# Attention scores as two 54-row passes on the two row halves of the matmul array, instead of one 110-row pass on the whole array

## The chip, the core and the metric

The kernel runs on one core of a Trainium2 chip. TensorE (PE) multiplies matrices, VectorE (DVE), ScalarE (ACT) and GpSimd (POOL) work on the results, SyncE (SP) issues most DMAs. The metric is the device time of one execution in microseconds (us). Smaller is better.

## What is computed

Two independent parts share the inputs' size (2048 positions, 576 features), and their outputs stand side by side:

```
# A: attention, 32 heads of 18 features, 4 segments of 512 positions
for s in range(4):
    logits = einsum("bhqd,bhkd->bhqk", q[s], k[s]) * 18**-0.5 + mask   # causal, within the segment
    a_dot  = einsum("bhqk,bhkd->bhqd", softmax(logits), v[s])
    a_mem  = (phi(q[s]) @ M) / (phi(q[s]) @ z + 1e-6)                  # M, z: sums over earlier segments
    out[s] = g * a_mem + (1 - g) * a_dot
    M += phi(k[s]).T @ v[s];  z += phi(k[s]).sum()
A = out @ wo
# B: a 2-D Fourier filter
B = irfft2(rfft2(x) * (w_r + 1j * w_i))
```

## The kernel before

The program is one stream per engine, in the order in which the Python code records it (a manual schedule). First come the forward transform of B and the projections to q, k and v; then the inverse transform of B, with the first steps of the attention in between (`prologue`); then the attention (`attention`), which takes the second half of the time.

For precision each value of q and k is held as three bf16 numbers (high, middle, low), and six of their nine products are kept. So a head's dot product over 18 features becomes one over 6 x 18 = 108 rows: `Qs` and `Ks` are tiles of 108 rows by 8 heads by 512 positions, and a matmul contracts all 108 rows. They are read back from DRAM by `stack_dmas`, three DMAs for a tile. Two more rows, 108 and 109, hold the maximum of each query (high and low part) and, on the key side, -1.

A *quad* is four heads of one segment; there are 32 quads (`k` = 0 to 31), and each takes four steps `t` of the attention loop, one per head. A step of the loop records these pieces, in this order:

- `s1` (line 688, the *maxima*) for a head 11 steps ahead: queries times keys over 108 rows into a PSUM tile of the pool `ps1` (three buffers, tag `s1`; while no background work asks for the buffer `post`, every fourth tile goes there), which DVE reads with the mask added and reduces to one maximum per query (line 692). A head has 1280 columns: one tile with 384 + 128 columns, one with 512, and every second head one with 256 + 256 for two heads.
- `s2` (lines 725 to 735, the *scores*): keys times queries, transposed, over 110 rows, so that the maximum is already subtracted, into one of three buffers `s2`; ACT takes the exponential (lines 726, 731, 736) into `P`. Also 1280 columns a head. Its matmuls alternate with those of `s1`.
- `run_bg`: one unit of background work at a time (`den`, `mixed`, `combine`, `mem1`, `oproj`: the memory part, the division, the output projection with `wo`), on the whole array, between two pieces of `s1` and `s2`.
- `pv` (line 763): the exponentials times the values, in fp32, four heads side by side on four column quarters of the array; a quad's products stand in two blocks, one in every second step, or for six quads in one block.
- `mpath`: in the steps 0 and 1 of a quad the maxima of the quad after next are split into high and low (POOL), transposed (PE, line 709, `mt`), copied (ACT), and sent by one DMA of ACT's queue into rows 108 and 109 of `Qs` (line 715).

PE's instructions wait in order for their semaphores; an instruction that waits holds up what stands behind it.

## Time and profile before

| | us |
|---|---|
| median of 3 runs (lowest, highest) | 673.66 (672.79, 673.68) |
| the profiled execution | 673.47 |
| its span, first to last instruction | 671.8 |
| PE busy | 658.6 (98%) |
| DVE busy | 543.2 (81%) |
| ACT busy | 440.6 (66%) |
| POOL busy | 189.6 (28%) |

The table's first rows are times of whole executions; the span is what the profile covers. A busy share is the union of an engine's instructions. Since matmuls are pipelined, the duration of one holds some fixed latency beside its streaming, so that a PE that is 98% busy can still lose time between matmuls; starts of neighbouring matmuls tell more than their durations.

### The profile page before, as it was taken

How to read it: one execution, taken by the hardware profiler on the slowest of the kernel's cores; microseconds unless marked ns; L12 is line 12 of the kernel's file. 1: busy time of each engine (PE TensorE's matmuls, PEld its weight loads, DVE VectorE, ACT ScalarE, POOL GpSimd, SP SyncE). 2: the span in 40 equal slices, each digit the busy share in tenths (PEclk: the TensorE clock that was granted, in tenths of full speed). 3: DMA queues.
4: the chain of work that ended last, by engine and by line, in shares of the span. 5: the costliest groups of instructions: out<-in, count | busy, mean ns of one | idle time of the engine just before them, and what ended most of it. 6: DMA issues, size and time to landing. Idle time of an engine off the chain costs nothing.

```text
span 671.8 us, 14143 instructions
## 1 busy us (share of the span) xinstructions
PE 658.6 (98%) x4776; PEld 484.3 (72%) x4776; DVE 543.2 (81%) x1514; ACT 440.6 (66%) x900; POOL 189.6 (28%) x387
## 2 busy tenths in 40 slices
PE   9999999999999999999999999999999999998997
PEld 5999779879879878999974454444666445663597
DVE  5998989889889778689769998998856988568643
ACT  3886796576487385444449988878756787567521
POOL 2111000100200012456506543445323564133410
PEclk9999999999999999999999999999999999999999
DMA  9896466497388478799545885876667576332152
GB/s 339 306 310 195 124 185 206 143 300 233 89 239 266 132 231 266 223 264 289 168 134 157 219 218 152 204 219 182 166 165 204 135 200 161 99 113 79 35 171 75
DMA packets 76034, 127.57 MB, mean 190 GB/s; under 512 B 12812, under 2 KB 44202, under 8 KB 72370
## 3 DMA queue, kind: packets, MB, share of 16 engines
q1 hardware_dynamic: 69310, 110.67, 57.3%
q0 software_dynamic: 5632, 15.76, 8.2%
q8 instruction: 37, 0.61, 0.4%
q10 hardware_dynamic: 1020, 0.25, 0.2%
q14 instruction: 35, 0.29, 0.1%
HBM read 81.78 MB, written 43.92 MB: 187 GB/s over the span
## 4 chain that ended last, share of the span: by engine, by line
PE 86%; DVE 5%; ACT 3%; DMA 3%; issue 2%; POOL 1%; SPq 0%; ACTq 0%; DVEq 0%; POOLq 0%
PE pj L487 15%; PE pv L763 11%; PE s L688 10%; PE pjv L487 7%; PE po L916 5%; PE i L331 4%; PE i L320 4%; PE f L145 4%; PE s L725 4%; PE c L166 4%; PE s L729 3%; PE pn L837 2%; PE s L735 2%; PE po L946 2%; PE pm L559 2%
## 5 line engine op out<-in xcount | busy, mean ns | idle before, releaser
L692 DVE CUSTOM_DVE_ANT_0 junk<-s,x 128x384 bf16<-128x384 f32 (+3 forms) x512 | 219.1, 486 | 42.2 <-PE s L688 39.7
L738 POOL TENSOR_SCALAR_AFFINE_SELECT P<-P 128x512 f32<-128x512 f32 (+2 forms) x135 | 80.6, 620 | 51.6 <-ACT P L726 47.3
L726 ACT ACTIVATE P<-s 128x512 f32<-128x512 f32 x128 | 76.7, 599 | 20.6 <-PE s L725 17.6
L763 PE MATMUL pv<-P,vs 128*32 128x512 f32 (+3 forms) x1024 | 81.0, 438 | 0.0
L731 ACT ACTIVATE P<-s 128x512 f32<-128x512 f32 x128 | 76.2, 596 | 3.4 <-PE s L730 3.0
L763 PEld LDWEIGHTS pv<-P,vs 128*32 128x32 f32 x1024 | 27.2, 109 | 44.0 <-issue 39.9
L688 PE MATMUL s<-Ks,Qs 108*128 108x512 bf16 (+3 forms) x256 | 57.7, 300 | 1.0 <-DVE mg L692 0.4
L487 PE MATMUL pj<-x,wqkh 128*128 128x512 f32 x162 | 56.1, 408 | 0.0
L232 DVE TENSOR_TENSOR Z<-Z 128x580 f32<-128x580 f32 (+2 forms) x51 | 45.9, 913 | 0.6
L692 DVE DVE_READ_ACCUMULATOR2_ANT mg<- 128x1 f32 x512 | 42.5, 83 | 0.0
L548 POOL MEMSET vt<- 128x32 f32 x16 | 2.3, 162 | 139.3 <-PE pm L559 125.5
L320 PE MATMUL i<-civ,Y 128*128 128x256 f32 (+1 forms) x288 | 39.7, 290 | 0.9 <-POOL Y L305 0.9
L736 ACT ACTIVATE P<-s 128x512 f32<-128x512 f32 x64 | 38.7, 605 | 2.5 <-PE s L735 1.1
L688 PEld LDWEIGHTS <-Qs 108*128 108x128 bf16 x320 | 26.9, 98 | 15.6 <-issue 11.0
L320 PEld LDWEIGHTS i<-civ,Y 128*128 128x128 f32 (+1 forms) x288 | 36.8, 181 | 1.9 <-POOL Y L305 1.3
L331 PE MATMUL i<-itab,T 128*128 128x290 f32 (+1 forms) x224 | 36.0, 304 | 0.1
L487 PE MATMUL pj<-x,wqkl 128*128 128x512 f32 x90 | 35.5, 395 | 0.0
L487 PE MATMUL pj<-xh,wqkh 128*128 128x512 f32 x90 | 35.5, 395 | 0.0
L487 PE MATMUL pj<-xh,wqkl 128*128 128x512 f32 x90 | 35.5, 395 | 0.0
L487 PEld LDWEIGHTS pj<-x,wqkh 128*128 128x128 f32 x162 | 30.5, 189 | 6.4
L506 DVE SCALAR_TENSOR_TENSOR ex<-pj,ex 128x512 f32<-128x512 f32 (+1 forms) x28 | 19.3, 689 | 19.5 <-ACT ex L504 19.4
L514 ACT CAST sp<-pj 128x512 bf16<-128x512 f32 x36 | 21.1, 585 | 18.6 <-DVE pj L507 18.4
(209 smaller groups left out, 1694.1 us busy)
## 6 DMA issues: line engine op xcount, KB each, us to landing
qkD<-sp SPq DMA_DIRECT2D x32, 384.0 KB
xin<-xb SPq DMA_DIRECT2D x16, 384.0 KB
cfw<-cfw POOLq DMA_DIRECT2D x16, 384.0 KB, 4.8
civ<-civ POOLq DMA_DIRECT2D x16, 384.0 KB, 8.3
Ks<-qkD SPq DMA_DIRECT2D x12, 512.0 KB
x<-qkD SPq DMA_DIRECT2D x10, 512.0 KB
Qs<-qkD SPq DMA_DIRECT2D x10, 512.0 KB
vs<-vD SPq DMA_DIRECT2D x16, 310.5 KB
```

The costliest lines, as they stand in the source:

```text
L232: s.nc.vector.tensor_tensor(o,a,b,op=op)
L320: nc.tensor.matmul(p[:m,k],Y[i][:,q,c*128:c*128+m],cc[:,hl,o:o+256],start=n==0,stop=n==5)
L331: nc.tensor.matmul(p,x,t,start=n==0,stop=n==6)
L487: s.nc.tensor.matmul(out,a,b,start=i==0,stop=i==len(L)-1)
L688: for o,i,e in J: nc.tensor.matmul(p[:,o:o+128*i+128],Q[:108,h+e,128*i:128*i+128],K[:108,h+e,:128*(i+1)],start=True,stop=True)
L692: nc.vector.tensor_tensor_reduce(out=junk[:,:w],in0=p[:,o:o+w],in1=s.mask[:,512-w:],scale=1.0,scalar=-3.0e38, op0=OP.add,op1=OP.max,accum_ ...
L726: nc.scalar.activation(P[0][:,hh],p0,AF.Exp,scale=SC)
L731: nc.scalar.activation(P[1][:,hh],p1,AF.Exp,scale=SC)
L736: nc.scalar.activation(P[2][:,hh-1:hh+1].rearrange("p h c -> p (h c)"),p2,AF.Exp,scale=SC)
L738: nc.gpsimd.affine_select(out=x[:,a:b],in_=x[:,a:b],pattern=[[0,b-a],[1,128]],compare_op=OP.is_ge,fill=0.0,base=0,channel_multiplier=-1)
L763: nc.tensor.matmul(s.pvt[32*hh:32*hh+32,128*j:],vt[:,152*j+19*h:152*j+19*h+32],mv[0][:,hh,mv[1]],start=j==0,stop=j>1,skip_group_check=True)
L916: nc.tensor.matmul(ps,a[t][:r,c],b[:r,t,w],start=i==0,stop=i==13)
```

## The change

A tile of queries or keys is now 56 rows of one row half of the array and 56 of the other: heads 0 to 3 of a group of eight lie in rows 0 to 55 (half 0), heads 4 to 7 in rows 64 to 119 (half 1). Each head's 108 rows are split in two parts of 54, which lie behind each other in the free dimension. A quad is now two heads of either half.

- The maxima (`fill`) use only one part of 54 rows, that with the leading products, so they are maxima of slightly rougher logits. Tiles are called A (384 + 128 columns), C (512) and B (256 + 256 for two heads); a quad has four A, four C and two B.
- The scores (`scores`, `s2`) take two passes that add up in PSUM: 56 rows (54 and the two of the maximum) and then 54. The exponentials are the same in number and size.
- `seg` replaces the alternation of `s1` and `s2` by a written list for each of the quad's four steps, with maxima of one or two quads ahead.
- `mpath` runs in steps 2 and 3 of the quad in place of 0 and 1, and sends two DMAs (one for each half) in place of one.
- `stack_dmas` issues four DMAs of 4 KB runs in place of three of 8 KB runs, with the same bytes.
- Background units of the output projection are taken two at a time in odd steps (`s.proj`), and `pv` stands in one block for quads 11 to 28. PSUM: four `s2` buffers, which `pv`, `mt`, `pn` and `po` now share, one buffer `x` for the rest, three `s1` buffers as before and none lent to them.
- The prologue does the maxima of two and a half quads in 15 calls (before: two and three quarters in 33).

In the order of PE's instructions the array changes between whole, row halves and column quarters 222 times in the attention (before 122) and 23 times in the inverse stage (before none).

```diff
-        L.append(lambda: nc.sync.dma_start(T[32:96].rearrange("p a c -> p (a c)"),s.qkD[g][u].rearrange("i (d h) c -> (i d) (h c)",h=8)))
...
+        for R in range(2):
+            m=bass.AP(tensor=a.tensor,offset=a.offset+2048*R,ap=[[65536,3],[4096,16],[65536,2],[1,2048]])
+            L.append(lambda R=R,m=m: nc.sync.dma_start(flat(T[64*R:64*R+48]),m))
+        def go(R):
+            m=bass.AP(tensor=e.tensor,offset=e.offset+(8*G+4*R)*512,ap=[[16384,6],[6*16384,2],[1,2048]])
+            nc.sync.dma_start(flat(T[64*R+48:64*R+54]),m)
...
-    def s1(s,t):
...
-            p=s.ps.tile([128,512],F32,name="s1",tag="post") if s.spare and s.n1%4==0 else s.ps1.tile([128,512],F32,name="s1",tag="s1")
-            for o,i,e in J: nc.tensor.matmul(p[:,o:o+128*i+128],Q[:108,h+e,128*i:128*i+128],K[:108,h+e,:128*(i+1)],start=True,stop=True)
...
+    def fill(s,k,kind,x):
+
+        nc=s.nc; n,qd=divmod(k,2); Q,K=s.Qs[n%3],s.Ks[n%4]; tp=s.sm; R=x//2 if kind!="B" else x
...
+        J={"A":[(0,2,x,384),(384,0,x,256)],"C":[(0,3,x,512)],"B":[(0,1,2*x,384),(256,1,2*x+1,256)]}[kind]
+        p=s.ps1.tile([128,512],F32,name="s1",tag="s1"); r=slice(64*R,64*R+54)
+        for o,i,hh,b in J:
+            j=2*qd+hh%2
+            nc.tensor.matmul(p[:,o:o+128*i+128],Q[r,0,j,128*i:128*i+128],K[r,1,j,:128*(i+1)],start=True,stop=True)
...
-        out=Q[108:110,4*qd:4*qd+4].rearrange("p h (i c) -> p (h i) c",c=128)
-        if s.now<0: nc.gpsimd.dma_start(out,mt)
-        else: s.later(2,lambda: nc.scalar.dma_start(out,mt))
+        def send(eng):
+            for R in range(2): eng.dma_start(Q[64*R+54:64*R+56,0,2*qd:2*qd+2].rearrange("p h (i c) -> p (h i) c",c=128),mt[16*R:16*R+16])
+        if s.now<0: send(nc.gpsimd)
+        else: s.later(2,lambda: send(nc.scalar))
...
+    def scores(s,p,n,J):
+
+        Q,K=s.Qs[n%3],s.Ks[n%4]; f=True
+        for b,rows in ((0,56),(1,54)):
+            for i,(o,h,kb,qo) in enumerate(J):
+                R,j=h//4,h%4; r=slice(64*R,64*R+rows)
+                s.nc.tensor.matmul(p[:,o:o+512-qo],K[r,1-b,j,128*kb:128*kb+128],Q[r,b,j,qo:],start=f,stop=b==1,skip_group_check=True)
+                f=False
+    def s2(s,k,kind,x):
+        nc=s.nc; n,qd=divmod(k,2); h=2*qd+(4*x if kind==2 else 4*(x//2)+x%2); tp=s.tp
...
+        p=s.ps.tile([128,512],F32,name="s2",tag="s2")
+        J={0:[(0,h,0,0)],1:[(0,h,1,128),(384,h,3,384)],2:[(0,h,2,256),(256,h+1,2,256)]}[kind]
+        s.scores(p,n,J)
+        nc.scalar.activation(P[2][:,2*x:2*x+2].rearrange("p h c -> p (h c)") if kind==2 else P[kind][:,x],p,AF.Exp,scale=SC)
+    def seg(s,t):
+
+        k,q=divmod(t,4)
+        L=(((0,0),("C",3),(0,2),("A",1)),((1,0),(1,2),("C",1),(2,1),("B",1),("B",0)),
+           ((0,1),("A",2),(0,3),("C",0)),((1,1),(1,3),("A",3),(2,0),("C",2),("A",0)))[q]
+        for a,x in L:
+            if a in (0,1,2):
+                if k<32: s.s2(k,a,x)
+            elif k+2+q//2<32: s.fill(k+2+q//2,a,x)
...
-        one=k in (16,17,18,24,25,26)
+        one=10<k<29
...
-        def run_bg(rate):
+        def run_bg(rate,t=1):
             state["acc"]+=rate
-            if state["acc"]>=1:
+            if t%2==0 and s.proj: return
+            while state["acc"]>=1:
...
-            steps(a,1)
-            steps(b,1)
-            run_bg(0)
-            steps(a,1)
-            steps(b,1)
-            run_bg(s.rate)
-            steps(a,1)
-            steps(b,1)
+            s.seg(t)
+            run_bg(s.rate,t)
             if 4<=t-1<132: s.pv((t-5)//4,(t-5)%4)
-            if hh==1 and m is not None: steps(m,2)
-            if hh==0 and k+2<32: m=s.mpath(k+2); next(m)
+            if hh==3 and m is not None: steps(m,2)
+            if hh==2 and k+2<32: m=s.mpath(k+2); next(m)
...
-                    tp=pool(es,"tp2",2); ps=es.enter_context(PP(tc,"ps",dict(s2=3,pv=1,post=1)))
+                    tp=pool(es,"tp2",2); ps=es.enter_context(PP(tc,"ps",dict(s2=4,x=1)))
```

PE in an early quad, first head of the quad, before (each LDWEIGHTS loads the weights of the MATMUL behind it; L688 is a maximum, L725 to L730 are scores; the last number is output rows x columns):

```order
L688 LDWEIGHTS Qs_3168
L688 MATMUL s_5450<-Ks_3169,Qs_3168 128x384
L688 LDWEIGHTS Qs_3168
L688 MATMUL s_5450<-Ks_3169,Qs_3168 128x128
L725 LDWEIGHTS x_2634
L725 MATMUL s_5457<-Qs_3167,x_2634 128x512
L688 LDWEIGHTS Qs_3168
L688 MATMUL s_5460<-Ks_3169,Qs_3168 128x512
L729 LDWEIGHTS x_2634
L729 MATMUL s_5464<-Qs_3167,x_2634 128x384
L730 LDWEIGHTS x_2634
L730 MATMUL s_5464<-Qs_3167,x_2634 128x128
```

Maxima and scores alternate, and each tile of scores is done by one matmul per 512, 384 or 128 columns. The same place now, the first step of a quad (L720 are scores, L689 maxima; `s_5852` belongs to a head of half 0, `s_5856` and `s_5860` to heads of half 1, `s_5864` to half 0):

```order
L720 LDWEIGHTS Ks_3171
L720 MATMUL s_5852<-Qs_3170,Ks_3171 128x512
L720 LDWEIGHTS Ks_3171
L720 MATMUL s_5852<-Qs_3170,Ks_3171 128x512
L689 LDWEIGHTS x_2634
L689 MATMUL s_5856<-Ks_3172,x_2634 128x512
L720 LDWEIGHTS Ks_3171
L720 MATMUL s_5860<-Qs_3170,Ks_3171 128x512
L720 LDWEIGHTS Ks_3171
L720 MATMUL s_5860<-Qs_3170,Ks_3171 128x512
L689 LDWEIGHTS x_2634
L689 MATMUL s_5864<-Ks_3172,x_2634 128x384
```

Two passes of one head stand directly behind each other on one half; a maximum of the other half follows.

ACT, from the exponentials of one quad (`P_4581`) to those of the next (`P_4737`), now (L708 copies the transposed maxima, L710 sends them):

```order
L710 DMA Qs_3169<-mts 2x8x128 x2
L729 ACTIVATE P_4582<-s_4610 128x512
L729 ACTIVATE P_4582<-s_4616 128x512
L729 ACTIVATE P_4583<-s_4626 128x512
L729 ACTIVATE P_4581<-s_4656 128x512
L729 ACTIVATE P_4581<-s_4668 128x512
L729 ACTIVATE P_4582<-s_4681 128x512
L729 ACTIVATE P_4582<-s_4687 128x512
L729 ACTIVATE P_4583<-s_4700 128x512
L654 CAST woh<-ob 128x576
L708 COPY mts<-mt 32x128
L772 COPY U<-pv 128x512
```

The two DMAs stand 8 exponentials ahead of the quad that needs them; before, the one DMA stood 13 exponentials ahead.

180 lines of the change are left out of this document (71 added, 109 removed).

## The prediction

> **What bounds the kernel now.** I read the page first: its span, the engines' shares, and the chain that ended last.
>
> ```profile
> span 671.8 us, 14143 instructions
> ...
> PE 658.6 (98%) x4776; PEld 484.3 (72%) x4776; DVE 543.2 (81%) x1514; ACT 440.6 (66%) x900; POOL 189.6 (28%) x387
> ...
> PE 86%; DVE 5%; ACT 3%; DMA 3%; issue 2%; POOL 1%; SPq 0%; ACTq 0%; DVEq 0%; POOLq 0%
> ```
>
> PE is the chain. The change touches the attention only, so I cut that by time: five quads without background work, five with light background, three with the output projection, and the end. The edges are starts of the transpose `mt`, one per quad; columns are PE, PEld, DVE, ACT, POOL, clock, DMA share, GB/s.
>
> ```profile
> 364.90:400.30 35.40, 35.40 (x329) 17.56 (x325) 34.04 (x164) 32.60 (x66) 19.57 (x35) 1.00 0.85 223
> 438.50:482.60 44.10, 44.08 (x343) 21.80 (x344) 40.11 (x171) 35.54 (x70) 21.69 (x39) 1.00 0.77 201
> 482.60:520.00 37.40, 37.33 (x327) 24.77 (x325) 23.24 (x101) 23.79 (x50) 11.46 (x26) 1.00 0.62 167
> 611.80:671.80 60.00, 54.73 (x407) 40.41 (x407) 31.24 (x48) 23.07 (x49) 12.06 (x25) 1.00 0.30 93
> ```
>
> A quad takes 7.08, 8.82 and 12.47 us in the first three. From 356.62 to 363.70 below is one of the early ones, 7.08. PE fills all of it; DVE stands at 96%, 91% and 62%. So in the first two there is a second engine close behind PE. How PE spends a quad shows in the timeline (start, duration):
>
> ```profile
> 356.62 1.28 PE L763 MATMUL pv<-P,vs 128*32 128x512 f32 x16
> ...
> 362.73 0.38 PE L725 MATMUL s<-Qs,Ks 110*128 110x512 bf16 x1
> 362.95 0.38 PE L688 MATMUL s<-Ks,Qs 108*128 108x512 bf16 x1
> 363.17 0.33 PE L729 MATMUL s<-Qs,Ks 110*128 110x384 bf16 x1
> 363.34 0.22 PE L730 MATMUL s<-Qs,Ks 110*128 110x128 bf16 x1
> 363.39 0.38 PE L735 MATMUL s<-Qs,Ks 110*128 110x256 bf16 x2
> 363.70 1.28 PE L763 MATMUL pv<-P,vs 128*32 128x512 f32 x16
> 364.92 0.23 PE L709 MATMUL mt<-idb,mh 128*128 128x128 bf16 x1
> 364.99 0.33 PE L688 MATMUL s<-Ks,Qs 108*128 108x384 bf16 x1
> ```
>
> Starts, not durations, give the cost: 512 columns take 0.22 us (362.73 to 362.95), of the 0.38 of a record 0.16 is latency. I call 512 columns a **unit**, 0.218 us. The two 256-column matmuls from 363.39 are one unit and end at 363.61, yet `pv` starts at 363.70: going from the whole array to column quarters costs **0.09**. A half block of `pv` takes 1.22 to the next start. A quad's maxima and scores are 20 units, 4.36; with 2 x 1.22, the first change of each block (2 x 0.09) and `mt` (0.07) that makes 7.05 of the 7.08.
>
> DVE's share in an early quad:
>
> ```profile
> 372.48 0.56 DVE L692 CUSTOM_DVE_ANT_0 junk<-s,x 128x384 bf16<-128x384 f32 x1 [0.19 <-PE s L688]
> ...
> 372.97 0.29 DVE L692 CUSTOM_DVE_ANT_0 junk<-s,x 128x128 bf16<-128x128 f32 x1
> ...
> 373.18 0.69 DVE L692 CUSTOM_DVE_ANT_0 junk<-s,x 128x512 bf16<-128x512 f32 x1
> ...
> 373.79 0.42 DVE L692 CUSTOM_DVE_ANT_0 junk<-s,x 128x256 bf16<-128x256 f32 x1
> ...
> 374.13 0.42 DVE L692 CUSTOM_DVE_ANT_0 junk<-s,x 128x256 bf16<-128x256 f32 x1
> ...
> 374.48 0.55 DVE L692 CUSTOM_DVE_ANT_0 junk<-s,x 128x384 bf16<-128x384 f32 x1
> ```
>
> By the starts a tile A (384 and 128) takes DVE 0.49 + 0.21 = 0.70, C 0.61, B 0.34 + 0.35 = 0.69. A quad (4 A, 4 C, 2 B) is **6.62 us of DVE**, and it was idle for 0.19 ahead of it, once in two heads. The change leaves this work as it is.
>
> **Do two halves run side by side?** No row shows row halves. The nearest is `pv`, four heads on four column quarters:
>
> ```profile
> L763 PE MATMUL pv<-P,vs 128*32 128x512 f32 x256 | 34.1, 605 | 0.0
> L763 PE MATMUL pv<-P,vs 128*32 128x384 f32 x256 | 27.2, 496 | 0.0
> ```
>
> 128 columns more cost 109 ns, so 512 fp32 columns stream in 0.44. There are 256 records for 128 matmuls: each fp32 product is two passes, and in the compiled stream the two passes of a head stand directly behind each other. If a pass that finds its quarter busy held up those behind it, the four heads' passes of 512 and of 128 would take 5 x 0.44 + 5 x 0.11 = 2.7 us. The 16 records from 363.70 take 1.22, twice 0.44 + 0.11 and a change. So the quarters advance independently, and I take the same for row halves.
> [...]
>
> **The change, part by part**, against the profiled execution's 673.5 (span 671.8 and 1.7 around it; the median of the runs, 673.7, is the same).
>
> *Streaming.* In units on half 0 and half 1 the four steps of `seg` hold 3 and 3, 4 and 5, 3 and 3, 5 and 4. Independent halves take 3 + 5 + 3 + 5 = 16 units in place of 20: -0.87 us of PE per quad.
>
> *Changes of the array.* 222 in place of 122 in the attention, about 3 more per quad. Whole to row halves is not shown; from 0 to the 0.09 of the column change. I take 0.09: +0.28 per quad, in projection quads (6 in place of 2) +0.37.
>
> *Feeding DVE.* This decides. Step 1 ends with C, B, B and step 3 with A, C, A, 1.99 and 2.01 us of DVE work, and three `s1` buffers hold just that. After the last of them PE feeds DVE nothing until the next quad's first maximum is complete. In an early quad that spell is 0.22 (last tile) + 0.09 + 1.22 (`pv`) + 0.07 + 0.09 (`mt`) + 0.44 (two passes of scores, which complete first) + 0.16 (latency) = 2.29; after step 1, without `mt`, 2.13. DVE is dry for 0.28 + 0.14 at least; as it has begun on the first tile before the third can be written, rather 0.65. While DVE has all three, PE waits, and the scores behind the waiting maximum wait with it. So an early quad takes between 7.04 and 7.4; I take 7.25: +0.17 for 11 quads (2 to 12), **+1.9**. PE's saving is not seen there, since DVE sets the time.
>
> In light quads (13 of those from 13 on) DVE has 40.11 / 5 = 8.02 busy against 34.04 / 5 = 6.81 before, so 1.2 more than 6.62. `pv` is one block there; two rows of the chain of waits give it and a background unit:
>
> ```profile
> 498.89 1.19 PE po L916 x7
> 500.31 2.29 PE pv L763 x32
> ```
>
> The spell without maxima becomes 0.22 + 0.09 + about 0.5 (a unit; 1.2 for one of `po`, less for `pb`) + 0.09 + 2.29 + 0.16 + 0.44 + 0.16 = 3.95, of which 2.0 is covered: dry 1.95. A quad by this loop: 6.62 + 1.2 + 1.95 = 9.8. PE alone would need 8.82 - 0.87 + 0.28 = 8.2. If part of the 1.2 falls into the dry spell it is 9.0; if PE and DVE wait for each other in turn, 10.4. I take 9.8: +1.0 x 13 = **+13** (ends -8 and +20).
>
> In the six projection quads PE has 12.47 - 0.87 + 0.37 = 12.0 and DVE 7.75 of work: PE sets the time, **-3**.
>
> *Start and end.* The prologue leaves 29.5 quads of maxima to the attention, before 29.25: 6.62 / 4 = **+1.7**. After the last maxima (2.5 quads) scores stand alone, 2 + 4 + 2 + 4 = 12 units in place of 10: 0.44 x 2.5, with the changes **+1.5**.
>
> *Rows of the maxima.* Before, the DMA that carries them left 9.67 us before the first use (the issue in ACT's timeline, the first scores of that quad in PE's):
>
> ```profile
> 373.20 0.62 ACTq L715 DMA_DIRECT2D Qs<-mts  x1
> ```
>
> ```profile
> 382.87 0.38 PE L725 MATMUL s<-Qs,Ks 110*128 110x512 bf16 x1
> ```
>
> Now two leave, 8 exponentials ahead in place of 13: 9.67 x 8 / 13 = 6.0 us, less 0.62 for the second. No wait for it shows today, and none is told of its landing; 0 to 7 us in all, I take **+1**. If the cover is gone, the first pass of every quad waits, and behind it everything on PE.
>
> *At nothing:* the loads of Q and K (same bytes, runs of 4 KB, one DMA more per tile on SP, whose queue waits mostly for the engines), the reordered stores of the projection, ACT's second issue (0.62, running beside an exponential; ACT has 35.40 - 32.60 = 2.8 free in five early quads, so it would cost 0.06 each if it did not overlap), the 23 changes in the inverse stage (2.1, against half or less of the maxima's streaming there).
>
> Sum: 1.9 + 13 - 3 + 1.7 + 1.5 + 1 = +16.1, from 673.5 to **690**.
>
> **Rivals.**
>
> *In order* (15%). A matmul that finds its half busy holds up the next. Then a step overlaps only where the half changes: 4 + 7.25 + 4 + 7.5 = 22.75 units, 0.60 more than before per quad. Early quads 7.08 + 0.60 + 0.09 = 7.77 (+7.6 for 11); light quads PE 8.82 + 0.88 = 9.7 with the loop at 9.8 or above, about 10.2 (+18); projection quads +0.97 each (+6); start, end and rows +4.2: +36, **709**. Against it: the 1.22 of `pv`; for it, that columns are not rows. [...]
>
> *Faster* (11%). The saved units come through: three buffers bridge the gaps, and DVE's other work falls into the dry spells. The point is a dry time below 1.0 us per light quad (8.82 - 7.82). Then early quads stay at 7.08, light ones take 8.82 - 0.87 + 0.37 = 8.3 (-0.5 x 13), the others -3, start and end +3: -6.5, **667**. For it: DVE's 91% and 62%, and the two heads' even spacing of work today; against it: 3.95 of `pv` and background in one piece.
>
> *Rows late* (8%). The DMAs land after their use in every quad of the early and light stretches by 0.4 us more than I took: +9, **699**. For it: two DMAs on queues at 85% DMA share; against it: 6 us.
>
> *No side by side at all* (4%): 30 units in place of 20, +2.18 and the changes for 29.5 quads, +73, **747**.
>
> *No difference* (3%): losses and gains cancel, 673.
>
> **How the numbers follow.** The forecast has 59% and its own range is 681 to 699 (light quads 9.3 to 10.4, early ones 7.04 to 7.4). The range of 8 in 10 reaches to the in-order case: 675 to 712; outside are the faster case, the 747 and half of the in-order case's far end. Below 0.2% (1.3 us) a measurement of this kernel cannot tell a difference. Faster 11%, same 3%, slower 86%.
>
> **What would show it.** Right: early quads of 7.2 to 7.4 (starts of `mt`), light quads of 9 to 10.4, DVE idle before the first maximum of a quad with PE as releaser, PE idle before the last maximum of steps 1 and 3 with DVE as releaser, two records of different halves starting within 0.01 us. Wrong: starts of a maximum only with the second pass ahead of it (in order); light quads below 8.8 (faster); PE waiting for the DMA of the maxima before the first pass of a quad (rows late); a change of whole array to halves that costs nothing would take up to 9 us (100 x 0.09) from the sum.

## The result, and the profile after

The changed kernel takes 727.87 us (median of 4 runs, 725.92 to 731.77) against 673.47 of the kernel before (four runs taken beside it): 1.082 times as long, 95% interval 1.077 to 1.087, or +54 us. The forecast was +16.5 us and a range up to 712, so the direction was right and the size was not. One of the four executions of `rows_by_pool` below lies 2% above its fastest, and its row is the median of the other three.

The page of the changed kernel: span, engines, and the chain of waits by engine and by line.

```profile
span 724.2 us, 15284 instructions
...
PE 682.5 (94%) x5288; PEld 490.1 (68%) x5288; DVE 543.0 (75%) x1514; ACT 432.7 (60%) x900; POOL 191.2 (26%) x389
...
PE 50%; DMA 13%; DVE 7%; ACT 6%; issue 5%; POOL 2%; SPq 1%; ACTq 1%; DVEq 0%; POOLq 0%
PE pj L487 10%; PE pv L766 7%; DMA Qs<-mts 6%; PE pjv L487 6%; PE s L720 6%; PE i L331 4%; PE i L320 4%; DVE junk L693 4%; PE po L912 4%; PE s L689 3%; ACT P L729 2%; DMA x<-mts 2%; PE po L942 2%; PE pm L559 2%; DMA vD<-vt 1%
```

PE was 86% of the chain and is 50%; DMA was 3% and is 13%, and 8% of it are two names that carry the rows of the maxima, `Qs<-mts` and `x<-mts` (the same tile under its first name). To see where the time went I cut both spans at the same starts of `mt`: first to third, third to thirteenth, thirteenth to seventeenth, seventeenth to last. First the kernel before (columns as in the prediction):

```profile
310.10:351.20 41.10, 39.84 (x302) 36.52 (x301) 30.78 (x102) 17.70 (x42) 16.17 (x25) 1.00 0.62 179
351.20:423.40 72.20, 71.31 (x650) 35.22 (x651) 68.03 (x326) 63.54 (x128) 34.15 (x64) 1.00 0.70 192
423.40:456.40 33.00, 32.42 (x273) 15.19 (x269) 31.82 (x138) 27.73 (x56) 16.21 (x34) 1.00 0.81 212
456.40:611.80 155.40, 153.30 (x1267) 88.71 (x1264) 118.44 (x501) 111.02 (x223) 63.80 (x114) 1.00 0.57 152
```

Then the changed one:

```profile
322.80:358.30 35.50, 33.85 (x245) 27.40 (x242) 26.34 (x95) 14.23 (x33) 10.11 (x17) 0.90 0.69 180
358.30:453.60 95.30, 81.06 (x827) 37.83 (x826) 69.73 (x330) 62.96 (x129) 36.38 (x67) 0.91 0.71 144
453.60:497.80 44.20, 36.60 (x339) 16.82 (x335) 33.60 (x142) 27.19 (x57) 17.25 (x34) 0.92 0.72 168
497.80:665.30 167.50, 159.32 (x1504) 89.96 (x1500) 117.29 (x495) 104.91 (x223) 60.61 (x111) 1.00 0.60 139
```

The span grew by 52.4: +7.1 up to the third `mt` (358.3 against 351.2), **+23.1** in the ten early quads, +11.2 in the next four, +12.1 in the last fifteen, and -1.1 in the tail (58.9 against 60.0). Two things are new in the stretches with the largest loss: PE stands still (81.06 busy of 95.30), and the granted clock, the share of full speed that PE was given, is 0.91 where it was 1.00. The intervals between starts of `mt` in the ten early quads are 8.28, 7.55, 11.32, 7.54, 10.87, 7.64, 14.96, 7.55, 12.08, 7.55. So there are two sorts of quad: a good one of 7.55, and a late one of 11 to 15. One late quad in the timeline (ACT's issues and PE):

```profile
367.65 0.62 ACTq L710 DMA_DIRECT2D Qs<-mts  x1
...
368.31 0.62 ACTq L710 DMA_DIRECT2D Qs<-mts  x1
...
374.11 0.23 PE L705 MATMUL mt<-idb,mh 128*128 128x128 bf16 x1
...
376.76 0.39 PE L720 MATMUL s<-Qs,Ks 56*128 56x512 bf16 x1 [2.42 <-DMA Qs<-mts]
```

The rows leave at 367.65 and 368.31, PE is ready for them at 374.34, and goes on at 376.76, 8.45 us after the second issue. The clock follows in the next rows, stretches of 3.4 us around that pause (the shortest pieces at half clock in this trace last 3.41 us):

```profile
371.40:374.80 3.40, 2.70 (x32) 1.15 (x26) 3.13 (x16) 3.14 (x8) 1.91 (x4) 1.00 1.05 165
374.80:378.20 3.40, 1.44 (x17) 0.85 (x18) 0.77 (x3) 1.05 (x3) 1.97 (x3) 1.00 1.03 210
378.20:381.60 3.40, 3.40 (x25) 1.15 (x22) 2.70 (x14) 1.92 (x4) 0.38 (x2) 0.50 0.63 125
381.60:385.00 3.40, 3.16 (x40) 1.69 (x40) 2.53 (x11) 2.67 (x6) 0.98 (x2) 1.00 0.55 159
```

PE was idle for about 2 of the 3.4 us from 374.80, and the next 3.4 us, in which it had work throughout, ran at half the clock. So this pause is followed by a second loss. Seven such pieces, 30.7 us in all, lie between 350 and 490 us, each right behind a pause of 0.85 us or more in the stretch before it; the kernel before has none ahead of its end. Its longest wait of PE between 350 and 500 us is this one (total, times, longest):

```profile
PE mt L709 <- DVE mg L692: 0.9, 1, 0.9
```

### The profile page after: what moved, and what is told of

The parts are those of the page before. It is cut to its first block, busy times and chain, and to the rows that moved or that the text cites. A ratio compares the mean times of both kernels' runs of the same rounds, so it can differ in the third digit from the quotient of the medians.

```text
span 724.2 us, 15284 instructions
## 1 busy us (share of the span) xinstructions
PE 682.5 (94%) x5288; PEld 490.1 (68%) x5288; DVE 543.0 (75%) x1514; ACT 432.7 (60%) x900; POOL 191.2 (26%) x389
## 4 chain that ended last, share of the span: by engine, by line
PE 50%; DMA 13%; DVE 7%; ACT 6%; issue 5%; POOL 2%; SPq 1%; ACTq 1%; DVEq 0%; POOLq 0%
PE pj L487 10%; PE pv L766 7%; DMA Qs<-mts 6%; PE pjv L487 6%; PE s L720 6%; PE i L331 4%; PE i L320 4%; DVE junk L693 4%; PE po L912 4%; PE s L689 3%; ACT P L729 2%; DMA x<-mts 2%; PE po L942 2%; PE pm L559 2%; DMA vD<-vt 1%
## 5 line engine op out<-in xcount | busy, mean ns | idle before, releaser
L729 ACT ACTIVATE P<-s 128x512 f32<-128x512 f32 x320 | 168.0, 605 | 54.9 <-PE s L720 33.0
L743 POOL TENSOR_SCALAR_AFFINE_SELECT P<-P 128x512 f32<-128x512 f32 (+1 forms) x131 | 78.9, 626 | 51.0 <-ACT P L729 50.3
L720 PEld LDWEIGHTS <-Ks 56*128 56x128 bf16 (+1 forms) x768 | 48.3, 96 | 52.6 <-issue 25.0
L720 PE MATMUL s<-Qs,Ks 56*128 56x512 bf16 (+7 forms) x512 | 66.9, 307 | 9.7 <-DMA Qs<-mts 7.1
L689 PE MATMUL s<-Ks,Qs 54*128 54x384 bf16 (+3 forms) x256 | 58.2, 309 | 5.1 <-DVE mg L693 5.1
L766 PEld LDWEIGHTS pv<-P,vs 128*32 128x32 f32 x1024 | 28.7, 112 | 50.1 <-issue 41.1
L232 DVE TENSOR_TENSOR Z<-Z 128x580 f32<-128x580 f32 (+2 forms) x51 | 45.9, 913 | 0.6
L689 PEld LDWEIGHTS <-Qs 54*128 54x128 bf16 x320 | 27.2, 96 | 19.5 <-issue 13.6
L720 PE MATMUL s<-x,Ks 56*128 56x128 bf16 (+7 forms) x256 | 33.2, 305 | 5.3 <-DMA x<-mts 5.0
L320 PE MATMUL i<-civ,Y 128*128 128x256 f32 (+1 forms) x288 | 37.1, 282 | 0.9 <-POOL Y L305 0.9
L708 ACT COPY mts<-mt 32x128 bf16<-32x128 bf16 x32 | 8.1, 254 | 49.0 <-PE mt L705 47.3
```

The source lines that it names most:

```text
L232: s.nc.vector.tensor_tensor(o,a,b,op=op)
L320: nc.tensor.matmul(p[:m,k],Y[i][:,q,c*128:c*128+m],cc[:,hl,o:o+256],start=n==0,stop=n==5)
L689: nc.tensor.matmul(p[:,o:o+128*i+128],Q[r,0,j,128*i:128*i+128],K[r,1,j,:128*(i+1)],start=True,stop=True)
L720: s.nc.tensor.matmul(p[:,o:o+512-qo],K[r,1-b,j,128*kb:128*kb+128],Q[r,b,j,qo:],start=f,stop=b==1,skip_group_check=True)
L729: nc.scalar.activation(P[2][:,2*x:2*x+2].rearrange("p h c -> p (h c)") if kind==2 else P[kind][:,x],p,AF.Exp,scale=SC)
L743: s.nc.gpsimd.affine_select(out=x,in_=x,pattern=[[0,4//b],[1,128]],compare_op=OP.is_ge,fill=0.0,base=0,channel_multiplier=-1)
```

## The experiments

The times in the second column are medians of three or four executions; ratios are to the kernel before, with 95% intervals. The last three columns come from the one profiled execution of each run. They are the time between starts of `mt`: third to thirteenth, thirteenth to seventeenth, seventeenth to last.

| run | us | ratio | early 10 | next 4 | last 15 |
|---|---|---|---|---|---|
| kernel before | 673.5 | 1 | 72.2 | 33.0 | 155.4 |
| changed kernel | 727.9 | 1.077 to 1.087 | 95.3 | 44.2 | 167.5 |
| no_row_wait | 722.1 | 1.066 to 1.075 | 83.9 | 46.5 | 174.9 |
| send_one_step_earlier | 734.9 | 1.088 to 1.094 | 91.7 | 44.8 | 181.5 |
| loads_after_rows | 725.2 | 1.076 to 1.080 | 94.2 | 44.0 | 167.4 |
| before_late_rows (old kernel) | 681.1 | 1.007 to 1.014 | 81.3 | 35.0 | 154.7 |
| no_rows | 707.3 | 1.046 to 1.055 | 77.2 | 47.4 | 163.9 |
| no_rows_one_pass | 708.8 | 1.044 to 1.056 | 77.8 | 51.8 | 164.3 |
| no_rows_half_max | 690.3 | 1.021 to 1.026 | 75.2 | 48.4 | 153.3 |
| rows_by_pool | 712.8 | 1.054 to 1.070 | 83.6 | 45.6 | 166.7 |
| no_loads | 716.0 | 1.060 to 1.065 | 77.1 | 44.4 | 174.5 |
| no_loads_no_rows | 715.4 | 1.059 to 1.067 | 77.5 | 42.7 | 173.4 |
| no_rows_no_sums | 699.3 | 1.035 to 1.040 | 76.9 | 40.4 | 165.5 |
| loads_8k | 732.0 | 1.086 to 1.093 | 92.1 | 46.1 | 172.2 |
| loads_64_32 | 715.4 | 1.058 to 1.065 | 85.5 | 48.3 | 165.3 |
| loads_64_at_0 | 720.5 | 1.068 to 1.074 | 88.1 | 43.9 | 165.9 |
| loads_96_rows | 721.0 | 1.067 to 1.072 | 90.9 | 45.9 | 165.4 |
| loads_96 | 984.1 | 1.457 to 1.469 | 169.6 | 93.5 | 300.4 |
| loads_32_16 | 748.6 | 1.107 to 1.115 | 95.7 | 50.3 | 183.7 |
| loads_32_16_pool | 727.2 | 1.074 to 1.081 | 90.8 | 52.7 | 169.2 |

### Is it PE's wait for the rows?

**no_row_wait**: the rows are sent to places that no pass reads.

```diff
-dma_start(Q[64*R+54:64*R+56,0,2*qd:2*qd+2]...
+dma_start(Q[64*R+58:64*R+60,0,2*qd:2*qd+2]...
-        for b,rows in ((0,56),(1,54)):
+        for b,rows in ((0,54),(1,54)):
```

> The changed kernel, with the DMAs of the maxima sent to rows that no matmul reads, and 54 rows in both passes of the scores: the subtraction of the maximum is left out, everything else stays, the two DMAs too. Theory late rows: the waits for these DMAs and the half clock that follows them are most of what was lost beyond the forecast. Early quads then all take 7.5 us (no more 11 to 15), the clock stays at 1.00, and the time falls to 690 to 700. Rival, the loop with DVE and the changes of the array cost it: the time stays above 715.

Only 6 of the 54 us came back, far from the 690 to 700 of the theory: the ten early quads fell by 11.4 us, and the last fifteen took 7.4 more. PE's own wait alone, as I had put it, is not the main cause of the whole. But the timeline shows that the row DMAs still held something, ACT this time:

```profile
401.50 0.62 ACTq L710 DMA_DIRECT2D x<-mts  x1
401.62 0.58 ACT L729 ACTIVATE P<-s 128x512 f32<-128x512 f32 x1
404.61 0.62 ACTq L710 DMA_DIRECT2D x<-mts  x1
405.33 3.04 ACT L729 ACTIVATE P<-s 128x512 f32<-128x512 f32 x6 [3.13 <-POOL mh L702]
```

The second DMA of the pair is issued 3.11 us after the first; ACT's exponentials stand behind it. (The releaser that the row names, POOL, is only what ended last by the profile.) The trace's records name the semaphores: the DMAs of SP and ACT use eight of them in turn (108, 110, 112 to 115, 117 and 118 in the changed kernel), and the DMA at 404.61 waits for the one that a background load, `pq`, used last. SP had issued that load among the loads of queries and keys, and its semaphore is complete at 404.59:

```profile
399.38 0.32 SPq L810 DMA_DIRECT2D pq<-pqD  x1
```

So this DMA of ACT left 0.02 us after the load that had used its semaphore was complete, and ACT's exponentials went on at 405.33.

**send_one_step_earlier** and **loads_after_rows** move the issue or the burst of loads by one step:

```diff
-        else: s.later(2,lambda: send(nc.scalar))
+        else: s.later(1,lambda: send(nc.scalar))
```

> The changed kernel with the DMAs of the maxima sent one step (about 1.8 us) earlier, nothing else. Theory late rows by a short lead: every late early quad gains up to 1.8 us, 5 of them 9 us, and some of the half clock is gone: 710 to 718. Rival, the DMAs land when the loads of queries and keys ahead of them are through, whatever the lead: if those loads are issued later than the rows now, the rows pass them and nearly all waits go (700); if they are not, nothing changes (728).

```diff
-            for _ in range(3 if t%8==0 else 1):
+            for _ in range(3 if t%8==1 else 1 if t%8 else 0):
```

> The changed kernel with the burst of three loads of queries and keys issued in the second step of a group of eight heads in place of the first, so that the rows of the maxima that are sent at the end of the first step are ahead of them. Theory late rows by collision (the rows land 7 to 11 us after their issue because they queue behind the loads): the rows land in 2 to 4 us, the early quads take 7.5, and the time falls to 693 to 703. Rival, the lead alone is too short: the time stays within 5 us of 728.

Earlier issue made it worse, outside every range expected: the intervals of the good quads went from 7.55 to 8.29, for a reason that I did not find, and late quads of 10.58, 12.46 and 10.25 stayed. Moving the burst left quads of 11.66, 11.75 and 15.05. But neither run brought the order that it was meant to test. In `loads_after_rows` the loads still left ahead of the rows (366.69 and 369.39 us, 384.81 and 385.53, 401.85 and 404.60), since in the trace the first of each group waits in SP's queue for a semaphore of PE, and the rows still landed up to 8.7 us after their issue. So these two runs say nothing against rows that stand behind loads.

**before_late_rows**: the kernel before, with `mpath` and its row DMA two steps later, where the changed kernel has them.

```diff
-            if hh==1 and m is not None: steps(m,2)
-            if hh==0 and k+2<32: m=s.mpath(k+2); next(m)
+            if hh==3 and m is not None: steps(m,2)
+            if hh==2 and k+2<32: m=s.mpath(k+2); next(m)
```

> The kernel before, whole array and one DMA for the rows, with the transpose and the send of the maxima two steps later in the quad, as the change has them. Theory: the later send alone makes the rows late, whatever the matmuls do; every other early quad loses 2 to 4 us and the clock drops: 685 to 700. Rival: one DMA on the old layout lands in 6 us at most and the lead of 6 us covers it: 673 to 677.

The old kernel loses about 7.6 us by this alone, between the two ranges expected. The early quads lose 9.1 (81.3 against 72.2, with quads of 8.54 and 13.24 where 7.08 stood), and the end gives some back. It shows the same half clock behind a pause:

```profile
399.90:403.30 3.40, 0.32 (x2) 0.21 (x3) 0.00 (x0) 0.00 (x0) 0.00 (x0) 1.00 0.55 131
403.30:406.70 3.40, 3.40 (x18) 1.55 (x20) 2.77 (x12) 2.16 (x4) 0.41 (x2) 0.50 0.54 149
```

So late rows and the halved clock belong to neither kernel; the old one kept clear of them by its lead.

### Rows, issues and loads apart

**no_rows**: neither sent nor read.

```diff
-        if s.now<0: send(nc.gpsimd)
-        else: s.later(2,lambda: send(nc.scalar))
...
-        for b,rows in ((0,56),(1,54)):
+        for b,rows in ((0,54),(1,54)):
```

> The rows of the maxima are not sent at all in the attention proper: neither of ScalarE's two DMAs per quad (L710) is issued, and both passes read 54 rows, so the maxima are not subtracted from the scores. Theory 'the rows' (now in a wider form): what the change lost beyond the forecast comes from these DMAs, by two ways: PE waits for their landing (14.3 us between 350 and 500 us of the changed kernel's span), and ScalarE, whose queue is in order, stands still when such a DMA may not be issued yet (in the run without the wait, the second of a pair left at 404.61, 3.1 us after the first, and ScalarE's exponentials stood behind it); each pause of PE of 0.85 us and more is followed by a piece of 3.4 us at half the clock. Without any of it: early quads 7.5 to 7.6 throughout, at most two pieces of half clock before the end, 692 us (685 to 700). Rival 'the work': the two passes themselves, or the fills that run two quads ahead, make PE stand still with the buffers as they are: then pauses and half-clock pieces stay, and the time stays at 715 to 722. Rival 'other DMAs': the loads or the background's own DMAs make the pauses: 705 to 720, with other transfers named at them.

The time is 707.3, outside the 685 to 700 of the theory and in the range of the rival 'other DMAs': in the early quads the theory holds (77.2, five intervals in a row of 7.54 to 7.55), in the next four it does not (47.4, below).

```profile
359.00:436.20 77.20, 74.44 (x828) 35.98 (x826) 69.09 (x330) 62.10 (x129) 36.43 (x67) 1.00 0.81 168
436.20:483.60 47.40, 38.87 (x339) 16.65 (x335) 33.40 (x142) 27.19 (x57) 17.45 (x34) 0.86 0.80 170
```

**no_loads** and **no_loads_no_rows** take the loads of queries and keys away instead, once with the rows and once without; the matmuls go on with what the start loaded.

```diff
-                if 0<n<14: q+=s.stack_dmas(n+2,0)
-                if 0<n<13: q+=s.stack_dmas(n+3,1)
+                if 0<n<14: s.loaded.add((n+2,0))
+                if 0<n<13: s.loaded.add((n+3,1))
```

> The changed kernel with its rows, but the queries and keys of the pairs of quads beyond the first ones are not loaded any more (the buffers keep what the start loaded, so the scores are those of other tiles): 384 and 48 KB transfers of L668 and L671 fall away, some 9 of 10 of SP's bytes in a pair of quads beside v. Theory 'the rows stand behind the loads': a pair of rows then lands 1.5 to 3 us after its issue each time instead of up to 10.8 us, no early quad waits, ScalarE is not held by an issue that waits for a load to end, and the time is that of no_rows or less: 700 to 708. If, beside that, the loads delay the background's own transfers (the pauses of 2 to 3.4 us before pb near 440 and 466 us in no_rows), these go too: 690 to 700. Rival 'the issues themselves' (two more DMAs a quad in ScalarE's queue, and what they wait for): the time stays at 715 or more, with late quads.

> As no_loads, and the rows are not sent either (54 rows in both passes; the maxima aren't subtracted). By 'the rows stand behind the loads' it is within 1% of no_loads; if it is 10 us or more faster than no_loads, the issue and the wait of the rows cost something of their own. Its time is that of PE, VectorE, ScalarE and their buffers: the forecast's terms for early quads (7.25) and light ones (9.8) without any transfer, about 690.

```profile
359.90:437.00 77.10, 74.48 (x829) 35.79 (x827) 69.16 (x330) 62.44 (x129) 36.48 (x67) 1.00 0.24 67
```

77.1 with the rows and without the loads, 77.2 without the rows and with the loads, 77.5 without both: in the early quads rows and loads cost nothing apart and 18 us together. In the packet records of ACT's queue a pair of rows of an early quad has landed 2.1 to 2.9 us after the first of its two issues without the loads, and up to 10.8 us after it with them. **Shown: the early loss is rows that stand behind loads.** The totals missed what was expected (716 and 715, not 700 to 708 and 690): two quads, at 529 and 621 us, took 17 to 18 us, with VectorE 7.0 us before `ry<-rD`, a transfer of the softmax's sums. Taking the loads away moved that transfer and its use closer together; I did not follow why.

**rows_by_pool**: GpSimd issues the rows at once.

```diff
-        if s.now<0: send(nc.gpsimd)
-        else: s.later(2,lambda: send(nc.scalar))
+        send(nc.gpsimd)
```

> The whole computation, with the two DMAs of a quad's rows issued by GpSimd at once behind the copy of the maxima instead of by ScalarE two steps later. Theory 'the rows': ScalarE is not held any more, and the rows leave about 3 us earlier, so the waits of PE (2 to 3.4 us in every second early quad) get shorter or vanish and with them the half clock: 690 to 710. If they leave as late for want of GpSimd (its selects stand in the same queue), 720 to 735. If the rows were not the cause, 728 as before.

The time is 712.8 (executions from 712.6 to 722.3), a little outside the 690 to 710 of the theory and better than the changed kernel. ACT is free, but a pair of rows still lands 2.3 to 7.9 us after its issue and PE waits 1.4 to 1.5 us in three early quads (9.01, 9.46, 10.73). So here the rows are late behind the loads from either engine.

**no_rows_no_sums**: in no_rows the four quads behind the early ones took 47.4. The two longest waits of PE and VectorE for a DMA between 350 and 500 us lie there:

```profile
PE pb L842 <- DMA rd<-rdD: 3.4, 1, 3.4
...
DVE ry L789 <- DMA ry<-rD: 3.0, 1, 3.0
```

```diff
-        nc.sync.dma_start(y,src.rearrange("h (b c) -> (h b) c",b=4))
+        nc.gpsimd.memset(y,1.0)
...
-        nc.sync.dma_start(r,dst)
+        nc.gpsimd.memset(r,1.0)
```

> As no_rows, and the softmax's sums are not brought back: the loads ry<-rD and rd<-rdD (once a head group, L786 and L803) are replaced by ones written by GpSimd, so nothing is divided by the sums. In no_rows VectorE stood 3.0 us before ry at 436.6 and PE 3.4 us before pb at 465.7, each followed by 6.8 us at half the clock, and the thirteenth to sixteenth quads took 47.4 us against 33.0 of the kernel before. Theory 'these two transfers': no pause of 2 us or more there, these four quads 38 to 40 us (light quads of 9.4 to 9.6), the time 695 to 700. Rival 'the background's own work there': they stay at 45 or more and the time at 705 to 708.

This is close to the theory of the two transfers: 40.4 (38 to 40 expected) and 699.3. Each transfer is used once a head group, its user stands still until it lands, and each pause is again followed by half the clock (6.8 us each in no_rows). In the changed kernel itself the wait for `rd<-rdD` is 3.0 us.

### What is left: streaming, maxima, buffers

```diff
 no_rows_one_pass:
-        for b,rows in ((0,54),(1,54)):
+        for b,rows in ((0,54),):
 no_rows_half_max:
-...tensor_tensor_reduce(out=junk[:,:w],in0=p[:,o:o+w],in1=s.mask[:,512-w:],...
+...tensor_tensor_reduce(out=junk[:,:w//2],in0=p[:,o:o+w//2],in1=s.mask[:,512-w:512-w//2],...
```

> As no_rows, and the second pass of the scores is left out as well (a kernel that computes too little: only the leading products stay). Ten blocks of 512 columns a quad less, in two halves side by side, are 5 x 0.218 = 1.1 us of PE a quad. If PE sets the light quads' time (9.4 in the changed kernel), they fall to about 8.3, and the early ones (7.55) to 6.6 or to VectorE's floor of 6.6; all 31 quads, 25 to 34 us less than no_rows. If VectorE or the loop of buffers sets the early quads, those stay at 7.5 and only the light ones move: 12 to 15 us less. If two halves do not in truth run side by side in the second pass, a quad loses 2.2 us and the time falls by 50 us or more.

> As no_rows, and each of VectorE's maxima reads only half of its columns (so the maxima are of too few scores). If VectorE or the loop through it sets the early quads (7.55), they fall to 6.5 or less; if PE sets them, they stay within 0.1. In the light quads likewise: 9.4 stays if PE sets it. The forecast's floor by VectorE (6.62) and its loop predict that the early quads move by less than 0.4 and the light ones by up to 0.8: 5 to 15 us less than no_rows.

The last fifteen intervals of no_rows, and of no_rows_half_max:

```profile
483.60:647.50 163.90, 157.27 (x1504) 89.26 (x1500) 117.22 (x495) 104.87 (x223) 60.34 (x111) 1.00 0.60 142
477.40:630.80 153.40, 152.03 (x1504) 89.04 (x1500) 80.44 (x495) 104.47 (x223) 61.45 (x112) 1.00 0.68 152
```

With half of VectorE's reading the early quads fall from 7.54 to 6.75 to 6.84, the shortest light ones from 9.38 to 8.43, and the kernel by 17 us, more than the 5 to 15 expected. So VectorE's maxima and the loop through them set both sorts of quad, and PE alone would need at most about 6.8 and 8.4; the forecast's PE floors were 7.05 - 0.87 + 0.28 = 6.5 and 8.2. With one pass less the early quads fall to 7.11, not to 6.6. Its light quads tell little: PE idles more, half-clock pieces add up to 65 us, and the total does not move. What a pass less may have saved there does not show behind that.

### Why the loads hold the rows up

Between 520 and 620 us the runs move the same bytes at almost the same rate (155 to 158 GB/s, but 150 in `loads_32_16` and 77 in `loads_96`), so the last but one column, the DMA engines' busy share, compares the loads. The changed kernel:

```profile
520.00:620.00 100.00, 96.58 (x930) 54.80 (x930) 70.21 (x305) 63.59 (x134) 38.88 (x69) 1.00 0.69 158
```

**loads_8k** asks whether the smaller packets do it; **loads_64_32** restores the old shape and place (64 rows on partitions 32 to 95, 32 rows on 0 to 31).

```diff
 loads_8k:
-            m=bass.AP(...,offset=a.offset+2048*R,ap=[[65536,3],[4096,16],[65536,2],[1,2048]])
+            m=bass.AP(...,offset=a.offset,ap=[[4096,48],[1,4096]])
 loads_64_32:
+            if n>3: w=(slice(32,96),slice(0,32))[R]; m=bass.AP(...,ap=[[4096,64-32*R],[1,4096]])
```

> The changed kernel, but each of the 48 rows that a query or key load (L668) brings is read as one piece of 8192 bytes instead of two of 4096 from two places (same rows of the buffers, same bytes, other data, so the scores are those of other queries and keys). Between 367 and 420 us a packet of 4096 bytes of the changed kernel took 346 ns in the mean, one of 8192 bytes of the kernel before 485 ns; the DMA engines were busy 0.85 to 0.92 of that time after and 0.69 before, at about the same GB/s. Theory 'the smaller packets fill the DMA engines, and the rows stand behind them': busy share there 0.70 to 0.75, rows land within 6 us, the quads from the third to the twelfth fall from 95.3 us together to 77 to 82 (77.2 without the rows), and the time to 705 to 715. If the loads are slow for another reason (48 partitions instead of 64, the place), the packets take twice as long and the late quads stay: 725 to 730.

> The changed kernel, but from the fifth pair of quads on the two loads of an operand (L668) have the shape of the kernel before: one of 64 rows on partitions 32 to 95 and one of 32 rows on partitions 0 to 31, 8192 bytes a row, instead of two of 48 rows on partitions 0 to 47 and 64 to 111 (same bytes; the queries and keys are others, and rows of the maxima are overwritten). A packet of 8192 bytes took 497 ns in the kernel before and 674 to 678 ns in the run whose loads of 48 rows were of 8192 bytes. Theory 'the loads are slower by the partitions that one of them covers': here 480 to 530 ns, the DMA engines' busy share between 420 and 520 us falls below 0.60 from 0.72, the rows land within 6 us from the quad at 400 us on, and the late quads go there: the time falls to 708 to 718. If the packets stay at 650 ns and more, the loads are slow for a reason that lies outside their shape (the other engines' traffic), and the time stays at 725 to 732.

```profile
520.00:620.00 100.00, 96.17 (x912) 54.07 (x909) 69.35 (x299) 62.94 (x134) 38.90 (x69) 0.98 0.69 155
```

That is loads_8k: share 0.69, 732 us. So it is not the packet size. And loads_64_32, 12 us faster than the changed kernel though the first pairs of quads still load as before:

```profile
520.00:620.00 100.00, 96.65 (x922) 54.71 (x921) 70.75 (x307) 64.30 (x136) 39.40 (x70) 1.00 0.55 156
```

This is about the same rate, 156 and 158 GB/s, for 0.55 of the engines' time in place of 0.69. Is it the number of rows or the place? **loads_32_16** splits each load of 48 rows into 32 and 16 (with the whole computation), **loads_64_at_0** puts the 64 rows on partitions 0 to 63 and the 32 on 64 to 95, **loads_96** and **loads_96_rows** use one load of 96 rows.

```diff
 loads_32_16:
+                for i,c in ((0,2),(2,1)):
+                    m=bass.AP(...,ap=[[4096,16*c],[65536,2],[1,2048]])
+                    nc.sync.dma_start(flat(T[64*R+16*i:64*R+16*i+16*c]),m)
 loads_64_at_0:
+            if n>3: w=(slice(0,64),slice(64,96))[R]; ...
 loads_96:
+                w=slice(0,96); m=bass.AP(...,ap=[[0,2],[4096,48],[1,4096]])
 loads_96_rows:
+                w=slice(0,96); m=bass.AP(...,ap=[[4096,96],[1,4096]])
```

> The whole computation of the changed kernel, with each load of 48 rows (L668) issued as one of 32 rows and one of 16 rows behind it (same places, same bytes in packets of 4096, twice as many loads). In the run whose loads were of 64 and 32 rows the median packet of 8192 bytes took 309 ns against 690 with 48 rows; in the changed kernel a packet of 4096 bytes took 329 ns in the median and 159 at best. If it is the number of 48 rows that makes the loads slow, the packets take 160 to 230 ns in the median, rows land within 6 us, and the time is 708 to 718. If it is that a load covers few partitions (under 64), the packets take 330 ns or more and the time is 725 to 735, more where the doubled issues hold SP and its semaphores.

> As the run with loads of 64 and 32 rows (from the fifth pair of quads on), but the 64 rows lie on partitions 0 to 63 and the 32 on 64 to 95, instead of 32 to 95 and 0 to 31. Same numbers of rows, same bytes, other place. Theory 'place': a load is fast where its partitions lie on both sides of 64, as 32 to 95 do; then these loads are as slow as those of 48 rows: packets of 8192 bytes 600 ns and more in the median (309 there), busy share of the DMA engines 0.70 or more between the thirteenth and sixteenth start of mt, time 725 to 732. Rival 'number': 64 rows are fast wherever they lie: 309 ns and 712 to 718. [...]

> As the run with 64 and 32 rows, but with one load of 96 rows on partitions 0 to 95 an operand (the second one of a pair falls away, and its place stays empty; same bytes). Theory 'the partitions that one load covers': the packets of 8192 bytes are at least as fast as with 64 and 32 rows, 430 to 500 ns, and the time is the same or up to 5 us less, 703 to 716. If the packet's time goes with the place of the rows and not with their number, it lies at 600 ns and more.

> One load of 96 rows on partitions 0 to 95 an operand from the fifth pair of quads on, now read from 96 neighbouring rows, so that the source's outermost dimension is 96 and not 2 as in the run that took 984 us (there two engines worked at a time, 16 us a load). By 'place' and by 'number' alike a packet takes 309 to 350 ns and the time is 703 to 716; if it is again above 900, the 96 partitions and not the source's outer dimension made that run slow.

```profile
520.00:620.00 100.00, 95.84 (x919) 55.09 (x912) 70.53 (x303) 63.06 (x134) 38.91 (x70) 1.00 0.62 156
```

That is loads_64_at_0: same rows and bytes as loads_64_32, another place, and 0.62 instead of 0.55; a packet of 8192 bytes takes 571 ns in the median instead of 309 (between 420 and 520 us; means 562 and 441), and the kernel 720.5 instead of 715.4 (the intervals of the ratio, 1.068 to 1.074 and 1.058 to 1.065, do not touch). So place counts. It is not all: 0.62 is still below the 0.69 of loads_8k, and I had expected 725 to 732. loads_32_16 made it worse (748.6; share 0.71 at 150 GB/s), and its packets of 4096 bytes take 314 ns in the median, so it is not the number 48 as such. loads_96_rows came out between (0.58, 721.0, not the 703 to 716 expected). So at 155 to 156 GB/s the shares are 0.55 with the 64 rows on 32 to 95, 0.62 with them on 0 to 63, and 0.69 with 48 rows on 0 to 47 and 48 on 64 to 111. The theory 'place' does not cover the second: by it these loads would have been as slow as those of 48 rows. What makes a place fast was not measured.

loads_96 is another matter: its source pattern had an outermost dimension of 2, in its packet records two engines work at a time, and a load takes 16 us. `loads_96_rows`, the same 96 partitions with 96 outermost in the source, takes 721.0 us in place of 984.1, so the source's pattern made that run slow and not the 96 partitions.

**loads_32_16_pool** joins two edits that keep the whole computation:

> As the one with 32 and 16 rows, and the rows of the maxima issued by GpSimd at once behind the copy of the maxima. If both help: 700 to 708. If the loads are as slow as before and only the issue of the rows helps: 715 to 720, as that change alone did.

It takes 727.2 us, outside both ranges and no better than the changed kernel. No version here beats the kernel before. One that loads both halves at once would need another arrangement in DRAM; it was not tried. The two loads of six rows (L671), which stand in place of one of twelve, were not varied. Nor was there a kernel that keeps PE busy through its pauses, so that the clock's share is read from order in time, not from an experiment of its own.

## Why the forecast was wrong, step by step

| step of the prediction | forecast | measured (span) |
|---|---|---|
| start, to the third `mt` | +1.7 | +7.1 |
| early quads (ten intervals) | +1.7 | +23.1 |
| the next four, light | +4 | +11.2 |
| the other nine light ones | +9 | +8.8 |
| six projection quads | -3 | +3.3 |
| end | +1.5 | -1.1 |
| rows of the maxima | +1 | in the rows above |

**The step that failed is "At nothing: the loads of Q and K (same bytes, runs of 4 KB, one DMA more per tile)", and with it "Rows of the maxima".** The lead that I worked out was about right: 6.0 us for the first DMA and 5.4 for the second, against 6.7 and 6.0 in the late quad above (issues at 367.65 and 368.31, PE ready at 374.34). But I took the landing for harmless because no row told of it, with the loads at no cost. The same bytes on other partitions fill the DMA engines more (0.69 against 0.55), and the rows that stand behind them are late. The shorter lead counts by itself: with the old loads it cost the old kernel 7.6 us. I called the bound 0 to 7 us, from one wait; it should have been a wait per quad, plus the clock. Rows and loads together cost 20.6 us of the total (727.9 less 707.3), 18.1 in the early quads of the profiled executions.

**The sums' transfers were no term either.** The next four quads lost 7 us more than forecast. Leaving `ry<-rD` and `rd<-rdD` out takes 7.0 us off these quads of no_rows and 8.0 off its time; in the changed kernel the wait for one of the two is 3.0 us. Why they are late with the change was not followed.

**The rival "rows late" had the right mechanism** and 8%, but at 0.4 us a quad it was priced at +9. It hits every second early quad from the third on, with waits of 2.2 to 3.4 us (one quad has a second one of 1.7) and 3.4 to 6.8 us at half the clock behind them. In the waits of PE between 350 and 500 us it heads the list:

```profile
PE s L720 <- DMA Qs<-mts: 9.3, 4, 2.4
PE s L689 <- DVE mg L693: 5.1, 16, 0.8
PE s L720 <- DMA x<-mts: 5.0, 2, 3.3
```

**The clock was no term at all.** Of the 30.7 us in the seven pieces half was not granted, about 15 us of PE at full speed. 3.4 of them lie in the start, about half of its +7.1. That is a sum over the records, and no run holds the clock fixed.

**Side by side held; in order is out.** Three rows of the timeline, and the same matmuls in the order in which `seg` records them:

```profile
400.10 0.39 PE L720 MATMUL s<-Qs,Ks 56*128 56x512 bf16 x1
...
400.11 0.39 PE L689 MATMUL s<-x,Qs 54*128 54x384 bf16 x2
...
400.33 0.39 PE L720 MATMUL s<-Qs,Ks 54*128 54x512 bf16 x2
```

```
L720 MATMUL s<-Qs,Ks 128x512      (half 0, first pass)
L720 MATMUL s<-Qs,Ks 128x512      (half 0, second pass)
L689 MATMUL s<-x,Qs  128x384      (half 1, a maximum)
L689 MATMUL s<-x,Qs  128x128
```

The maximum of half 1 starts at 400.11, before the second pass of half 0 at 400.33, which stands ahead of it in the program. So the halves advance independently here, as taken from `pv`. The rival 'in order', in which a matmul that finds its half busy holds up the next, does not hold across row halves here.

**The light quads were right in size.** Nine undisturbed ones took 9.38 to 10.52, 89.1 us together against 80.3 before: +0.98 each where I had +1.0, by the loop I named (PE waits for `DVE mg` 16 times in the list above, and half the maxima take 0.9 us off). **The good early quads** take 7.55, above my 7.25 and the end of 7.4. The missing 0.3 need not be the three buffers. In the ten early quads of no_rows VectorE's longest waits are two, and the sum has no term for the second:

```profile
DVE junk L693 <- PE s L718: 3.4, 8, 0.4
DVE junk L693 <- POOL mh L701: 3.1, 8, 0.6
```

In eight of the ten quads a maximum waits about 0.4 us for a semaphore of GpSimd's cast of the maxima; between 351 and 423 us the kernel before shows no such wait. No run takes it out, so its share stays open. **The six projection quads** took 74.8 in no_rows, 78.3 in the changed kernel and 75.1 before: the saving of 3 does not appear even undisturbed. The end was mis-sized by 2.6, and what is left of the start, about 2 us beyond the forecast's 1.7, stays open.

## What to carry to other kernels

A transfer that "moves the same bytes" is not the same transfer: here the place of its rows changed how long it filled the DMA engines (a share of 0.55 or 0.62 for the same 64 and 32 rows), and a small transfer with a short lead paid for it. When an engine has no slack, price a stall as its wait plus what the clock takes afterwards; here a pause of 2.4 us came with a quad longer by 3.8 us. An experiment that moves a line of the program has to show in the trace that the order of issue moved too. And before costing an edit at nothing, look at what queues behind it: on the same DMA engines, and on the same engine that issues (ACT's exponentials stood 3.1 us behind one issue).

## What was not expected of the hardware

- **The clock halved after short pauses.** Pauses of 0.85 to 3.4 us were followed by 3.4 to 6.8 us at 0.50 in the changed kernel, by up to 13.7 in no_rows_one_pass. In the changed kernel the stretch of 3.4 us ahead of a piece was idle for a third to four fifths, seven times. It is no fixed rule: a pause of 2.0 us at 622.43 us, of which 1.5 lie in one such stretch, was not followed by a fall, nor was the 0.9 of the kernel before.
- **Place of a load.** Between 420 and 520 us, 8192-byte packets took 309 ns in the median (441 in the mean) on partitions 32 to 95 with 0 to 31 (loads_64_32), 571 (562) on 0 to 63 with 64 to 95 (loads_64_at_0), and 678 (674) on 0 to 47 with 64 to 111 (loads_8k). The number goes with the traffic too: on the first of these places the kernel before, at 190 in place of 154 GB/s, has 440 (497).
- **An issue held its engine.** In no_row_wait a DMA of 4 KB on ACT's queue kept ACT's exponentials waiting for 3.1 us: it left at 404.61 us, and its semaphore was owed until 404.59 by a background load that SP had issued 5.2 us before.
